# Transposing x and q by DMA instead of on TensorE in a sorted block attention with a maxout layer

## The chip, the cores and the metric

The kernel runs on one core of a Trainium2 chip. The metric is the time of one execution on the device, in microseconds (us); for the kernel before it is 178.51 us, the median of three runs (178.17 to 178.69). A profile of one execution, which spans 176.5 us on the core, gives what each engine did and when. The engines are TensorE (PE in the profile, with its weight loads as PEld), VectorE (DVE), ScalarE (ACT), GpSimd (POOL) and SyncE (SP); SP here only issues transfers. Matmul results land in PSUM, of which this kernel makes four buffers, and some other engine has to move ("evict") each to SBUF.

## The reference, cut to what matters

Four items (the batch), eight heads, 768 tokens, head size 64. Each head's tokens fall into 8 blocks of 96. A small matrix P (8x8 for each head, made doubly stochastic by five rounds) mixes the blocks of k and of v; then each block of queries attends to its mixed block; the result is, token by token, the x of a layer with two input matrices, a maximum, and an output matrix.

```python
for _ in range(5):
    P = P - np.max(P, axis=-1, keepdims=True)
    P = np.exp(P)
    P = P / (np.sum(P, axis=-1, keepdims=True) + 1e-09)
    P = P / (np.sum(P, axis=-2, keepdims=True) + 1e-09)
k_sorted = np.einsum('bhij,bhjcd->bhicd', P, k_b)      # the same for v
scores = scale * np.matmul(q_b, k_sb.transpose(0, 1, 2, 4, 3))
attn = softmax(scores)                                  # written out in the reference
x = np.matmul(attn, v_sb)                               # -> (4*768 tokens, 512)
h1 = x @ w1
h2 = x @ w2
out = np.maximum(h1, h2) @ w_out
```

## The kernel before

The kernel uses max(h1, h2) = relu(x(w1-w2)) + x w2, so the output is relu(x(w1-w2)) w_out + x (w2 w_out). All products are bf16. The program is a fixed order of instructions: for each item, 20 or 24 "units" on TensorE (eight products h, twelve halves of output tiles; item one has four products of weights as well), and between the units "steps" of the attention of the next item. The parts that the change touches (cuts are marked `...`):

```python
# queries: paired by heads on VectorE, transposed on TensorE, evicted
def pair_q(b, two):
    if two == 0:
        q_pair[b] = qpool.tile([128, HP, R, 2 * D], BF16, tag="q_pair", name="q_pair", bufs=1)
    nc.vector.tensor_copy(out=q_pair[b][..., two * D : (two + 1) * D], in_=...)  # q_raw[b]

def q_transposes(b, half, eng=None, n=0):
    ...
    for m in range(2 * R):                       # 12 of 128x128
        ...
            nc.tensor.matmul(ps[:, c], q_pair[b][:, hp, r], ident, is_transpose=True, ...)
    ...
    evac(qT[b][:, half * 2 : half * 2 + 2]..., ps[:, 0 : 2 * R * 128], ...)

# scores of four blocks and two heads, then the exponent
def scores(b, u, n=0):
    ih, hp = divmod(u, HP)
    ps = ps_f32("s_ps")
    ...
            rhs = qT[b][rows, hp, :, i * PB : (i + 1) * PB]      # R x PB = 6 x 16 tokens
            nc.tensor.matmul(
                ps[:, h2 * 512 + ii * BLK : h2 * 512 + (ii + 1) * BLK],
                kT[b][rows, ...], rhs, start=True, stop=True,
            )
    e = e_bufs[(b * 8 + u) % NE]
    nc.scalar.activation(out=e[...], in_=ps[0:BLK]..., func=AF.Exp, scale=scale)

# values; x is divided by the sum of its row as it leaves PSUM
def values(b, u, n=0):
    ...   # 8 matmuls o_ps <- e, v_sb
    nc.vector.reciprocal(out=rs, in_=ov[:, :, :, 64])
    if hp % 2 == 0:
        x_tiles[b, ih, hp // 2] = xpool.tile([BLK, 2, 4, 2, D], BF16, tag="x", name="x", bufs=3)
    ...
    nc.vector.tensor_tensor(out=x, in0=ov[:, :, :, 0:D], in1=rs..., op=ALU.mult)

# x transposed on TensorE; its eviction puts the tokens in order
def x_transposes(b, t, eng=None):
    ih, hh = divmod(t, 2)
    ps = ps_bf16("tx_ps")
    x = x_tiles.pop((b, ih, hh))
    for m in range(8):                           # 8 of 96x128
        ...
    dst = xT[:, b % 2, ih, hh].rearrange("p h (i c r) -> p h i c r", r=R, c=PB)
    src = ps.rearrange("p (h f) -> p h f", h=2)[:, :, 0:TCH].rearrange("p h (i r c) -> p h i c r", r=R, c=PB)
    evac(dst, src, 2 * TCH, eng=eng)

# products h of unit t of chunk ch (384 tokens): reads w1_sb and xT, evicted as g
def moe_h_products(b, ch, t, hps, n=0): ...
# half an output tile of 128 tokens: reads g and wo_sb, xT and wc
def moe_out(b, ti, part): ...                    # every fourth half evicts o and stores it from SP

# the order: steps of the next item, and what hangs behind a unit by its number
tail = {..., 9: [pair_q(1, 0), pair_q(1, 1), load_q(2), load_v(2), load_v(3)],
        16: [block_diagonals(2)], 18: [block_diagonals(3)]}       # lambdas left out
for b in range(B):
    ...
    tail = {0: [VA[6], VA[7]], 1: [TR[2]], 2: [TR[3]]}            # behind the next item's first units
    if b == 0:
        tail[3] = [load_k(3)]
        tail[8] = [load_q(3)]
```

SC, VA and TR are the scores (8 for an item), values (8) and transposes of x (4; the first two feed chunk 0, the others chunk 1). Items are numbered from 0 in the code; the text says item one for b = 0. Bulk loads of q, k, v and the weights go from GpSimd's queue and cast fp32 to bf16 on the way; the stores of the output go from SP's.

Of the kernel before, what the change touches and what calls it, by code (L numbers as in the profile page):

```python
# [9 lines left out]

FP32 = mybir.dt.float32
BF16 = mybir.dt.bfloat16


@with_exitstack
def kernel(
# [16 lines left out]
    nc = tc.nc  # L33
# [4 lines left out]
    B, H, S, D = q.shape  # L38
    NB = sort_net.shape[-1]
    BLK = S // NB  # L40
# [5 lines left out]
    R = S // 128  # L46
    PB = 128 // NB
    HP = H // 2
    HB = BLK // 2
    TCH = S // 2  # L50
# [152 lines left out]
    def turn_v(rows, eng, c0, c1, d0=0, d1=D):  # L203
        dst = v_dc[rows, 0 : D * BLK].rearrange("p (d c) -> p d c", c=BLK)[:, d0:d1, c0:c1]
        src = v_raw[rows].rearrange("p (c d) -> p d c", d=D)[:, d0:d1, c0:c1]
        if eng == "A":
            nc.scalar.copy(out=dst, in_=src)
        else:
            nc.vector.tensor_copy(out=dst, in_=src)  # L209


    rowsum = const.tile([G, NB], FP32, tag="rowsum", name="rowsum")
# [116 lines left out]
        )  # L329
        load["D"] += 900  # L330

    def q_transposes(b, half, eng=None, n=0):

        if half == 0:
            qT[b] = qpool.tile([128, HP, R, 128], BF16, tag="qT", name="qT")
        ps = ps_f32("tq_ps") if n else ps_bf16("tq_ps")
        keep_streaming(ps, n)
        if n:
            ps = ps.bitcast(BF16)
        for m in range(2 * R):  # L340
            hp, r = half * 2 + m // R, m % R
            c = slice(m * 128, (m + 1) * 128)
            if b in q_pair:
                nc.tensor.matmul(  # L344
                    ps[:, c], q_pair[b][:, hp, r], ident, is_transpose=True, start=True, stop=True
                )
                continue
            for h2 in range(2):
                nc.tensor.matmul(  # L349
                    ps[h2 * 64 : h2 * 64 + 64, c],  # L350
                    q_raw[b][:, hp + 4 * h2, r * D : (r + 1) * D],
                    ident,
                    is_transpose=True,
                    start=True,
                    stop=True,
                )
# [78 lines left out]
        keep_streaming(ps, n)  # L435
        for ii in range(4):
            i = ih * 4 + ii
            for h2 in range(2):
                rows = slice(h2 * 64, h2 * 64 + 64)
                rhs = qT[b][rows, hp, :, i * PB : (i + 1) * PB]  # L440
                nc.tensor.matmul(  # L441
                    ps[:, h2 * 512 + ii * BLK : h2 * 512 + (ii + 1) * BLK],
                    kT[b][rows, (hp * 8 + i) * BLK : (hp * 8 + i) * BLK + 128],
                    rhs,
                    start=True,
                    stop=True,
                )
        e = e_bufs[(b * 8 + u) % NE]
        nc.scalar.activation(  # L449
            out=e[:, 0 : 8 * BLK].rearrange("p (t f) -> p t f", t=2),  # L450
            in_=ps[0:BLK].rearrange("p (t f) -> p t f", t=2)[:, :, 0 : 4 * BLK],
            func=AF.Exp,
            scale=scale,
        )
        load["A"] += 800
        e_tiles[b, u] = e

    def values(b, u, n=0):
        ih, hp = divmod(u, HP)
        e = e_tiles.pop((b, u))  # L460
        m0 = (b % 2) * 64
        ps = ps_f32("o_ps")
        keep_streaming(ps, n)
        for h2 in range(2):
            for ii in range(4):
                nc.tensor.matmul(  # L466
                    ps[:, h2 * 512 + ii * 65 : h2 * 512 + (ii + 1) * 65],
                    e[:, (h2 * 4 + ii) * BLK : (h2 * 4 + ii) * BLK + 128],
                    v_sb[:, m0 + (hp + 4 * h2) * 8 + ih * 4 + ii, 0:65],
                    start=True,  # L470
                    stop=True,
                )
        ov = ps[0:BLK].rearrange("p (t f) -> p t f", t=2)[:, :, 0 : 4 * 65].rearrange(
            "p t (i f) -> p t i f", f=65
        )
        rs = xpool.tile([BLK, 2, 4], FP32, tag="rs", name="rs")
        nc.vector.reciprocal(out=rs, in_=ov[:, :, :, 64])  # L477
        if hp % 2 == 0:
            x_tiles[b, ih, hp // 2] = xpool.tile(
                [BLK, 2, 4, 2, D], BF16, tag="x", name="x", bufs=3  # L480
            )
        x = x_tiles[b, ih, hp // 2][:, :, :, hp % 2, :]
        nc.vector.tensor_tensor(  # L483
            out=x,
            in0=ov[:, :, :, 0:D],
            in1=rs.to_broadcast([BLK, 2, 4, D]),
            op=ALU.mult,
        )
        load["D"] += 900

    def x_transposes(b, t, eng=None):

        ih, hh = divmod(t, 2)
        ps = ps_bf16("tx_ps")
        x = x_tiles.pop((b, ih, hh))
        for m in range(8):
            h2, ii = divmod(m, 4)
            nc.tensor.matmul(  # L498
                ps[:, h2 * 1024 + ii * BLK : h2 * 1024 + (ii + 1) * BLK],
                x[:, h2, ii].rearrange("p n d -> p (n d)"),  # L500
                ident[0:BLK, 0:BLK],
                is_transpose=True,
                start=True,
                stop=True,
            )
# [192 lines left out]
    def load_rest():  # L698
# [18 lines left out]
        9: [  # L717
            lambda: pair_q(1, 0),
            lambda: pair_q(1, 1),
            lambda: load_q(2),  # L720
            lambda: load_v(2),
            lambda: load_v(3),
        ],
        16: [lambda: block_diagonals(2)],
        18: [lambda: block_diagonals(3)],
    }
    for b in range(B):
        units = [lambda t=t: moe_h(b, 0, t, None if b else "A") for t in range(4)]
        if b == 0:
# [21 lines left out]
            ]  # L751
        steps, lo = [], 2
        if b < B - 1:
            qs = [lambda half=half: q_transposes(b + 1, half) for half in range(2)]
            pairs = [lambda two=two: pair_q(b + 1, two) for two in range(2)]
            ks = [lambda t=t, b=b: sort_k(b + 1, t) for t in range(3)]
            SC, VA, TR = att(b + 1)

            def group(*fs):
                return [lambda: [f() for f in fs]]  # L760

            if b == 0:
                lo = 10
                tail[9][2:2] = ks
                vs = [lambda t=t: sort_v(1, t) for t in range(4)]
                tns = [lambda c=c: turn(both, c) for c in range(0, BLK, 12)]
                VA[1:6] = [(lambda f=f, g=g: (f(), g())) for f, g in zip(VA[1:6], tns)]
                TR[0:2] = [(lambda f=f, g=g: (f(), g())) for f, g in zip(TR[0:2], tns[5:])]
                SC[7:] = [lambda f=SC[7], g=tns[7]: (f(), g())]
                steps = group(*vs[:3]) + qs[:1] + group(*SC[0:2], vs[3]) + qs[1:] + VA[:1]  # L770
                steps += group(*SC[2:5]) + VA[1:2]
            elif b == 1:
                vs = [lambda t=t: sort_v_pair(2, t) for t in range(8)]
                steps = group(*pairs) + group(*ks) + qs[:1] + group(*SC[0:2], vs[0]) + qs[1:]
                steps += group(*vs[1:4]) + group(*vs[4:7]) + group(*SC[2:4], vs[7]) + VA[:2]
            else:
                steps = group(*pairs) + group(*ks) + qs + group(*SC[0:2])
# [19 lines left out]
_INS = ['q', 'k', 'v', 'sort_net', 'moe_w1', 'moe_w2', 'moe_w_out']  # L797
_OUTS = [((3072, 512), 'float32')]
# [25 lines left out]
```

The softmax here doesn't subtract the row's maximum and nothing guards it: scores larger than these inputs give would overflow.

## Time and profile before

| what | value |
|---|---|
| time, median of 3 runs | 178.51 us |
| span of the profiled execution | 176.5 us |
| granted TensorE clock | 1.00 throughout |
| matmuls L593 (output tiles) | 208 + 104 instructions, 48.1 + 25.0 us busy |
| matmuls L566 (h) | 256 instructions, 45.8 us busy |
| matmuls L498 (transposes of x) | 128 instructions, 8.1 us busy |
| matmuls L344 and L349 (transposes of q) | 72 and 48 instructions, 4.8 and 1.7 us busy |
| exponents on ScalarE, L449 | 32 instructions, 24.2 us busy |
| moved from and to HBM | 25.17 MB read, 6.29 MB written |

How to read it: "busy" adds the durations of an engine's instructions, where overlapping ones count once. Matmuls are pipelined: the next begins before the one ahead of it has ended, so a group's mean duration is longer than what one more of its kind adds to the time. A row of a group reads: line of the kernel, engine, operation, output <- inputs, shapes, count | busy us, mean ns of one | idle us of the engine just ahead of them, and what ended most of that idle time. The chain of work that ended last is followed back from the last instruction, at each step to what released it, or to the instruction ahead of it on its engine. Row "DMA" of the slices gives in tenths how busy the 16 DMA engines were in each fortieth of the span.

### The profile page before, as it was taken

The page shows a single profiled execution, that of the slowest core. Times are in us where ns is not written, and L with a number is a line of the kernel's source. Part 1 is how long each engine was busy: PE and PEld are TensorE (multiplying, and loading weights), DVE is VectorE, ACT ScalarE, POOL GpSimd, SP SyncE. Part 2 cuts the span into 40 slices and gives each one's busy share as a digit, 9 for nine tenths or more (in the row PEclk, how much of TensorE's full clock was granted, in tenths as well). Part 3 has the DMA queues.
Part 4 walks back from the last instruction along what each step waited for, and adds up shares of the span by engine and source line. Part 5 has one row for each costly group of instructions (what it writes and reads, how often), then busy time and mean ns, then how long its engine had stood idle before and what let it go on. Part 6 is the DMA issues. An engine that isn't in the chain of part 4 may idle for free.

```text
span 176.5 us, 4808 instructions
## 1 busy us (share of the span) xinstructions
PE 169.4 (96%) x2159; PEld 105.1 (60%) x2159; DVE 95.3 (54%) x201; ACT 91.1 (52%) x110; POOL 24.1 (14%) x39
## 2 busy tenths in 40 slices
PE   7999999999999999999989999999999999999993
PEld 7848675655765554577655454677555546654453
DVE  4979758688555697354586435346325426240210
ACT  3689957854663655277783341474833232630021
POOL 7855353110730000020000000000000000000000
PEclk9999999999999999999999999999999999999999
DMA  4999999999799962039200203300001132000333
GB/s 55 200 205 208 198 207 215 201 203 210 114 214 212 206 176 108 16 119 148 38 0 4 97 26 119 119 6 4 0 0 62 61 119 111 12 0 0 119 116 125
DMA packets 13940, 19.19 MB, mean 109 GB/s; under 512 B 800, under 2 KB 8864, under 8 KB 13920
## 3 DMA queue, kind: packets, MB, share of 16 engines
q0 software_dynamic: 10304, 12.58, 42.4%
q1 hardware_dynamic: 3328, 6.10, 9.1%
q8 instruction: 17, 0.28, 0.6%
q10 hardware_dynamic: 288, 0.20, 0.3%
q14 instruction: 3, 0.02, 0.0%
HBM read 25.17 MB, written 6.29 MB: 178 GB/s over the span
## 4 chain that ended last, share of the span: by engine, by line
PE 84%; DVE 9%; ACT 4%; issue 1%; DMA 1%; ACTq 0%
PE out_ps L593 36%; PE h_ps L566 23%; PE o_ps L466 4%; PE k_ps L374 4%; PE wc_ps L544 4%; PE tx_ps L498 3%; PE s_ps L441 3%; PE tq_ps L344 2%; PE v_ps L395 2%; DVE g L582 1%; ACT w2T L103 1%; PE tw_ps L521 1%; DMA p_sb<-in_sort_net_dram 1%; PE tq_ps L349 1%; DVE x L483 1%
## 5 line engine op out<-in xcount | busy, mean ns | idle before, releaser
L593 PE MATMUL out_ps<-wo_sb,g 128*128 128x512 bf16 (+2 forms) x208 | 48.1, 363 | 0.3 <-DVE g L582 0.2
L566 PE MATMUL h_ps<-xT,w_sb 128*128 128x384 bf16 x256 | 45.8, 326 | 0.4 <-DVE g L582 0.2
L566 PEld LDWEIGHTS <-w_sb 128*128 128x128 bf16 x256 | 23.8, 98 | 15.1 <-issue 0.2
L449 ACT ACTIVATE e<-s_ps 96x768 bf16<-96x768 f32 x32 | 24.2, 803 | 12.2 <-PE s_ps L441 12.0
L580 ACT ACTIVATE g<-h_ps 128x768 bf16<-128x768 f32 x22 | 17.7, 811 | 21.8 <-PE h_ps L566 21.7
L593 PEld LDWEIGHTS <-g 128*128 128x128 bf16 x208 | 17.9, 97 | 15.9 <-issue 0.2
L593 PE MATMUL out_ps<-wc,xT 128*128 128x512 bf16 (+2 forms) x104 | 25.0, 362 | 0.0
L103 ACT COPY o<-out_ps 128x1024 f32<-128x1024 f32 x8 | 8.1, 1013 | 29.3 <-PE out_ps L593 25.6
L483 DVE TENSOR_TENSOR x<-o_ps,rs 96x512 bf16<-96x512 f32 x32 | 22.0, 687 | 1.1
L477 DVE RECIPROCAL rs<-o_ps 96x8 f32<-96x8 f32 x32 | 6.4, 201 | 25.5 <-PE o_ps L466 25.4
L582 DVE TENSOR_SCALAR g<-h_ps 128x768 bf16<-128x768 f32 x10 | 9.6, 957 | 15.7 <-PE h_ps L566 15.6
L593 PEld LDWEIGHTS <-xT 128*128 128x128 bf16 x104 | 9.9, 97 | 10.9
L209 DVE COPY v_dc<-v_raw 64x768 bf16<-64x768 bf16 (+2 forms) x18 | 15.6, 897 | 0.5 <-DMA v_raw<-in_v_dram 0.4
L466 PEld LDWEIGHTS <-e 96*128 96x128 bf16 x256 | 11.0, 98 | 5.6 <-ACT e L449 0.5
L466 PE MATMUL o_ps<-v_sb,e 96*128 96x65 bf16 x256 | 12.4, 193 | 0.3 <-DVE x L483 0.2
L103 ACT COPY xT<-tx_ps 128x768 bf16<-128x768 bf16 x13 | 10.4, 798 | 4.5 <-PE tx_ps L498 4.5
L105 DVE CAST v_sb<-v_ps 96x1024 bf16<-96x1024 f32 x7 | 8.5, 1215 | 5.3 <-PE v_ps L395 3.3
L103 ACT CAST v_sb<-v_ps 96x1024 bf16<-96x1024 f32 x9 | 8.7, 1014 | 2.3 <-PE v_ps L395 1.4
L103 ACT CAST kT<-k_ps 128x1024 bf16<-128x1024 f32 x10 | 9.6, 1026 | 0.5 <-PE k_ps L374 0.5
L441 PEld LDWEIGHTS <-kT 64*128 64x128 bf16 x256 | 6.1, 94 | 5.4 <-issue 4.6
L129 POOL DMA_DIRECT2D q_raw<-in_q_dram x4 | 3.6, 902 | 39.8 <-DVE q_pair L326 37.4
L81 PEld LDWEIGHTS <-fill 128*128 128x128 bf16 x109 | 7.7, 128 | 2.2 <-DVE fill L72 1.2
(77 smaller groups left out, 166.1 us busy)
## 6 DMA issues: line engine op xcount, KB each, us to landing
out_dram<-o SPq DMA_DIRECT2D x11, 512.0 KB, 2.8
k_raw<-in_k_dram POOLq DMA_DIRECT2D x12, 256.0 KB, 14.0
q_raw<-in_q_dram POOLq DMA_DIRECT2D x4, 768.0 KB, 9.7
v_raw<-in_v_dram POOLq DMA_DIRECT2D x6, 384.0 KB, 12.5
w_sb<-in_moe_w_dram POOLq DMA_DIRECT2D x3, 512.0 KB, 15.7
wo_sb<-in_moe_w_out_dram POOLq DMA_DIRECT2D x2, 512.0 KB, 19.4
v_raw<-in_v_dram POOLq DMA_DIRECT2D x3, 256.0 KB, 5.1
w_sb<-in_moe_w_dram POOLq DMA_DIRECT2D x2, 256.0 KB, 14.3
```

Of the source, the lines that this page charges most:

```text
L81: nc.tensor.matmul(ps[:, 0:w], w0, fill[:, 0:w], start=True, stop=True)
L103: nc.scalar.copy(out=out_ap, in_=in_ap)
L105: nc.vector.tensor_copy(out=out_ap, in_=in_ap)
L209: nc.vector.tensor_copy(out=dst, in_=src)
L441: nc.tensor.matmul(ps[:, h2 * 512 + ii * BLK : h2 * 512 + (ii + 1) * BLK], kT[b][rows, (hp * 8 + i) * BLK : (hp * 8 + i) * BLK + 128], rhs ...
L449: nc.scalar.activation(out=e[:, 0 : 8 * BLK].rearrange("p (t f) -> p t f", t=2), in_=ps[0:BLK].rearrange("p (t f) -> p t f", t=2)[:, :, 0 ...
L466: nc.tensor.matmul(ps[:, h2 * 512 + ii * 65 : h2 * 512 + (ii + 1) * 65], e[:, (h2 * 4 + ii) * BLK : (h2 * 4 + ii) * BLK + 128], v_sb[:, m0 ...
L483: nc.vector.tensor_tensor(out=x, in0=ov[:, :, :, 0:D], in1=rs.to_broadcast([BLK, 2, 4, D]), op=ALU.mult,)
L566: nc.tensor.matmul(h_ps[t][:, m * 512 : m * 512 + TCH], w1_sb[:, hp, fb * 128 : (fb + 1) * 128], xT[:, b % 2, ch, hp % 2, hp // 2, :], sta ...
L580: nc.scalar.activation(out=g, in_=src, func=AF.Relu)
L582: nc.vector.tensor_scalar(out=g, in0=src, scalar1=0.0, scalar2=None, op0=ALU.max)
L593: nc.tensor.matmul(dst, g_tiles[b, ch, m // 2][:, m % 2, off : off + 128] if m < NFB else xT[:, b % 2, ch, hp % 2, hp // 2, off : off + 12 ...
```

## The change

For items two to four the normalised x, and for items three and four the queries, no longer go through TensorE and an eviction: a DMA from the SP queue transposes them from SBUF to SBUF. It is meant to relieve TensorE of the transposes, and VectorE and ScalarE of their evictions. [...]the exponent now reads the scores in the order of tokens. Around this the order is changed: the transposes are started as early as their data is there, the last two values of an item are computed ahead of the item boundary, the loads of v for items three and four go ahead of the q of item three, and the loads of k and q of item four wait for the first scores of item three, so that no bulk load runs near the transposes. `TWICE = 1` leaves the copies of v as they are.

```diff
-    def q_transposes(b, half, eng=None, n=0):
+    def q_transposes(b, half, eng=None):
 
         if half == 0:
             qT[b] = qpool.tile([128, HP, R, 128], BF16, tag="qT", name="qT")
-        ps = ps_f32("tq_ps") if n else ps_bf16("tq_ps")
-        keep_streaming(ps, n)
-        if n:
-            ps = ps.bitcast(BF16)
+        if b > 1:
+            nc.sync.dma_start_transpose(
+                out=qT[b][:, half * 2 : half * 2 + 2].rearrange("p h r c -> p (h r) c"),
+                in_=q_pair[b][:, half * 2 : half * 2 + 2].rearrange("p h r e -> p (h r e)"),
+            )
+            return
+        ps = ps_bf16("tq_ps")
... scores
-                    ps[:, h2 * 512 + ii * BLK : h2 * 512 + (ii + 1) * BLK],
+                    ps[:, h2 * 512 + ii * 128 : h2 * 512 + ii * 128 + BLK],
...
-            out=e[:, 0 : 8 * BLK].rearrange("p (t f) -> p t f", t=2),
-            in_=ps[0:BLK].rearrange("p (t f) -> p t f", t=2)[:, :, 0 : 4 * BLK],
+            out=e[:, 0 : 8 * BLK].rearrange("p (t c r) -> p t c r", t=8, r=R),
+            in_=ps[0:BLK].rearrange("p (t f) -> p t f", t=8)[:, :, 0:BLK].rearrange(
+                "p t (r c) -> p t c r", r=R
+            ),
... values
-                [BLK, 2, 4, 2, D], BF16, tag="x", name="x", bufs=3
+                [BLK, 2, 4, 2, D], BF16, tag="x", name="x", bufs=4
... x_transposes
+        if b > 0:
+            nc.sync.dma_start_transpose(
+                out=xT[:, b % 2, ih, hh].rearrange("p h (i c) -> p (h i) c", c=BLK),
+                in_=x.rearrange("p h i n d -> p (h i n d)"),
+            )
+            return
...
-        dst = xT[:, b % 2, ih, hh].rearrange("p h (i c r) -> p h i c r", r=R, c=PB)
-        src = ps.rearrange("p (h f) -> p h f", h=2)[:, :, 0:TCH].rearrange(
-            "p h (i r c) -> p h i c r", r=R, c=PB
-        )
-        evac(dst, src, 2 * TCH, eng=eng)
+        src = ps.rearrange("p (h f) -> p h f", h=2)[:, :, 0:TCH]
+        evac(xT[:, b % 2, ih, hh], src, 2 * TCH, eng=eng)
... the order
-            lambda: load_q(2),
             lambda: load_v(2),
             lambda: load_v(3),
+            lambda: load_q(2),
         ],
-        16: [lambda: block_diagonals(2)],
-        18: [lambda: block_diagonals(3)],
+        22: [lambda: block_diagonals(2)],
+        23: [lambda: block_diagonals(3)],
     }
+    def late_loads():
+
+        held = const.tile([1, 1], BF16, tag="held", name="held")
+        nc.gpsimd.tensor_copy(out=held, in_=e_tiles[2, 0][0:1, 0:1])
+        load_k(3)
+        load_q(3)
...
-            pairs = [lambda two=two: pair_q(b + 1, two) for two in range(2)]
+            if b < 2:
+                tail[18 - 4 * b] = [lambda two=two: pair_q(b + 2, two) for two in range(2)]
+                tail[18 - 4 * b] += [lambda half=half: q_transposes(b + 2, half) for half in range(2)]
...
-                steps = group(*pairs) + group(*ks) + qs[:1] + group(*SC[0:2], vs[0]) + qs[1:]
+                steps = group(*ks) + group(*SC[0:2], vs[0], late_loads)
...
-            steps += VA[2:3] + TR[:1] + VA[3:4]
-            steps += group(*rest[:-1]) + TR[1:2] + VA[4:5] + rest[-1:] + VA[5:6]
+            steps[-1:] = group(VA[1], TR[0])
+            steps += VA[2:3] + group(VA[3], TR[1])
+            steps += group(*rest[:-1]) + VA[4:5] + rest[-1:] + group(VA[5], TR[2])
+            steps += VA[6:7] + group(VA[7], TR[3])
...
-        tail = {0: [VA[6], VA[7]], 1: [TR[2]], 2: [TR[3]]}
-        if b == 0:
-            tail[3] = [lambda: load_k(3)]
-            tail[8] = [lambda: load_q(3)]
+        tail = {}
```

More of the change, by code (lines that the diff above doesn't have):

```diff
@@ L12 @@
 BF16 = mybir.dt.bfloat16
+TWICE = 1
 @with_exitstack
@@ L205, in turn_v @@
         src = v_raw[rows].rearrange("p (c d) -> p d c", d=D)[:, d0:d1, c0:c1]
[L206 to L209, printed above, removed]
+        for _ in range(TWICE):
+            if eng == "A":
+                nc.scalar.copy(out=dst, in_=src)
+            else:
+                nc.vector.tensor_copy(out=dst, in_=src)
     rowsum = const.tile([G, NB], FP32, tag="rowsum", name="rowsum")
@@ L493, in x_transposes @@
         ih, hh = divmod(t, 2)
+        x = x_tiles.pop((b, ih, hh))
+        if b > 0:
[4 more added lines that the diff above has]
+            return
         ps = ps_bf16("tx_ps")
-        x = x_tiles.pop((b, ih, hh))
         for m in range(8):
@@ L753 @@
         if b < B - 1:
-            qs = [lambda half=half: q_transposes(b + 1, half) for half in range(2)]
-            pairs = [lambda two=two: pair_q(b + 1, two) for two in range(2)]
+            qs = [lambda half=half: q_transposes(1, half) for half in range(2)]
+            if b < 2:
+                tail[18 - 4 * b] = [lambda two=two: pair_q(b + 2, two) for two in range(2)]
+                tail[18 - 4 * b] += [lambda half=half: q_transposes(b + 2, half) for half in range(2)]
             ks = [lambda t=t, b=b: sort_k(b + 1, t) for t in range(3)]
@@ L773 @@
                 vs = [lambda t=t: sort_v_pair(2, t) for t in range(8)]
-                steps = group(*pairs) + group(*ks) + qs[:1] + group(*SC[0:2], vs[0]) + qs[1:]
+                steps = group(*ks) + group(*SC[0:2], vs[0], late_loads)
                 steps += group(*vs[1:4]) + group(*vs[4:7]) + group(*SC[2:4], vs[7]) + VA[:2]
             else:
-                steps = group(*pairs) + group(*ks) + qs + group(*SC[0:2])
+                steps = group(*ks) + group(*SC[0:2])
                 steps += VA[:1] + group(*SC[2:5]) + VA[1:2]
             rest = SC[4:] if b == 1 else SC[5:]
-            steps += VA[2:3] + TR[:1] + VA[3:4]
-            steps += group(*rest[:-1]) + TR[1:2] + VA[4:5] + rest[-1:] + VA[5:6]
+            steps[-1:] = group(VA[1], TR[0])
+            steps += VA[2:3] + group(VA[3], TR[1])
+            steps += group(*rest[:-1]) + VA[4:5] + rest[-1:] + group(VA[5], TR[2])
+            steps += VA[6:7] + group(VA[7], TR[3])
         done = 0
```

## The prediction

> **What bounds the kernel now.** I read the busy table and the slices first, then the chain of work that ended last, then the groups, and last the DMA issues. The busy table, and the slices of the same page:
>
> ```profile
> PE 169.4 (96%) x2159; PEld 105.1 (60%) x2159; DVE 95.3 (54%) x201; ACT 91.1 (52%) x110; POOL 24.1 (14%) x39
> ...
> PE   7999999999999999999989999999999999999993
> ...
> DMA  4999999999799962039200203300001132000333
> ```
>
> TensorE is full in every slice but the first and the last; VectorE and ScalarE are half idle; the DMA engines are full until about 62 us (14 slices of 4.4 us), and after that in spells: a load of q at 79 to 84 us, and the stores. Matmul busy time is overlapping time, so 96% alone doesn't say that TensorE is the bound. The chain does:
>
> ```profile
> PE 84%; DVE 9%; ACT 4%; issue 1%; DMA 1%; ACTq 0%
> PE out_ps L593 36%; PE h_ps L566 23%; PE o_ps L466 4%; PE k_ps L374 4%; PE wc_ps L544 4%; PE tx_ps L498 3%; PE s_ps L441 3%; PE tq_ps L344 2%; PE v_ps L395 2%; DVE g L582 1%; ACT w2T L103 1%; PE tw_ps L521 1%; DMA p_sb<-in_sort_net_dram 1%; PE tq_ps L349 1%; DVE x L483 1%
> ```
>
> Most of the DVE share is the Sinkhorn start (the first 12.6 us). After it, the set end is TensorE work laid end to end, and the transposes (L498 of x, L344 of q) are links of that chain, not work beside it. The same chain in order of time, around the start of item two (start, us, what):
>
> ```profile
> 75.22 1.30 PE h_ps L566 x8
> 76.52 0.34 PE tx_ps L498 x8
> 76.86 1.30 PE h_ps L566 x8
> 78.16 0.34 PE tx_ps L498 x8
> 78.50 1.64 PE k_ps L374 x96
> 80.14 1.41 PE h_ps L566 x8
> 81.55 0.67 PE tq_ps L344 x12
> ```
>
> Here a transpose costs its steady price: eight of x take 0.34 us (42 ns each), twelve of q 0.67 us (56 ns), with nothing idle before or behind. These are the prices to use, not the groups' mean of about 0.2 us for one, which contains its latency.
>
> **What the Trainium skill says.** (1) "VectorE: DVE Perf Modes", section "The three transpose paths", gives a 128x128 bf16 transpose 390 ns on TensorE and 1309 ns by the DMA crossbar. Back to back this trace has 56 ns for the first, seven times less: the page's figure is for one alone. A DMA transpose has no trace here. (2) "DMA: Bandwidth & Descriptors", section "Latency and other measured facts", gives DMA transposes 261 GB/s with a non-contiguous middle dimension. No run shows this yet. (3) The same page, section "Rules for kernel authors": issue a DMA early and wait late, so that its fixed cost overlaps; and a transpose beside ordinary DMAs needs no ordering. The trace agrees with a fixed cost, in the last row of these DMA issues (KB each, median us from issue to landing):
>
> ```profile
> out_dram<-o SPq DMA_DIRECT2D x11, 512.0 KB, 2.8
> ...
> p_sb<-in_sort_net_dram SPq DMA_DIRECT2D x1, 8.0 KB, 1.7
> ```
>
> An 8 KB load on the SP queue needs 1.7 us, nearly all of it fixed.
>
> **The change part by part.** Removed from TensorE: the transposes of x for three items, 3 x 4 calls of 8, 12 x 0.34 = 4.1 us; those of q for two items, 2 x 2 calls of 12, 4 x 0.67 = 2.7 us (the chain has 0.67, 0.67 and 1.34). All of it lies on the path. Sum 6.8 us.
>
> Removed from the half-idle engines, with the evictions' own rows:
>
> ```profile
> L103 ACT COPY xT<-tx_ps 128x768 bf16<-128x768 bf16 x13 | 10.4, 798 | 4.5 <-PE tx_ps L498 4.5
> ...
> L105 DVE COPY qT<-tq_ps 128x1536 bf16<-128x1536 bf16 x7 | 6.6, 953 | 1.8 <-PE tq_ps L344 1.1 <-PE tq_ps L349 0.7
> ```
>
> Twelve evictions of xT (0.80 us on ScalarE, 0.95 on VectorE) and four of qT (0.95, one of them 1.44 on ScalarE), some 14 us over the two engines. It is worth time only where TensorE waits for a PSUM buffer. Between 83 and 91 us the chain leaves TensorE three times for an eviction of g (0.82, 0.97, 0.97 us); TensorE has scores and sorted values to run meanwhile, so it stands idle only 0.2 to 0.3 us each time. Two qT evictions fall in this stretch, but the transposes that kept TensorE busy go too. I credit 0.3 us.
>
> Added: the SP queue gets 12 transposes of 96x1024 (197 KB) and 4 of 128x1536 (393 KB). Estimated from the 1.7 us above and the page's 261 GB/s: 1.7 + 0.75 = 2.5 us and 1.7 + 1.5 = 3.2 us. Off the path, if the result isn't needed sooner. The tightest consumers, with times of the kernel before:
> - Last x of item two. Its values now run ahead of the last two halves of an output tile, about 70.6 us; by the row of x (687 ns) behind such a call it is ready at 71.9. Its reader is the fifth product h of item two, at 84.4, or about 82.4 when the transposes and the two moved calls of values in between are taken out. Slack 10 us.
> - x for the first chunk of item two: ready near 62.8, read at 73: slack 10 us.
> - q of item three: paired near 66.9, read by the scores near 82: slack 15 us.
> If the queue moves one transpose at a time, with T for an x and 2T for a q half, four T of q and two of x stand between 66.9 and some 80.6 us (1.8 us of landing left over): T may be up to 2.3 us, that is 197 KB / 2.3 us = 85 GB/s. The page's rate is three times that. Item three gives nearly the same (q paired near 105, last x read near 119.5), and item four has no q behind it.
>
> Changed without cost: the exponent now reads PSUM with a step of 16 fp32, where it read in order (803 ns for 768). The eviction of kT reads with a step of 64 fp32 and takes 1026 ns for 1024 elements, the one of o reads in order and takes 1013: on ScalarE the step costs nothing here. The eviction of item one's xT becomes an ordered one, 0.80 us as before.
>
> Moved: the values of the last two units go ahead of the item boundary, 2 x 0.24 us merely moved. The loads of v for items three and four go ahead of q for item three: the two v are 1.5 MB, q 0.8 MB, issued from about 45 us; at the 205 GB/s of those slices they are through at 45 + 11.5 + 2 = 58.5 us, just ahead of the first DMA transpose (x ready near 59.7), and q is used at 65. k and q of item four wait for the first scores of item three (about 82 us), and need 1.5 MB / 205 GB/s = 7.5 us more with 2.6 us of issuing: landed near 92 to 94, while q is paired near 100. So no new wait from loads.
>
> Sum: 178.5 - 6.8 - 0.3 = 171.4 us. As some of the slack is estimated and new groupings cost a pipeline break of 0.1 us here and there, I say 172.0.
>
> **Rivals.** (a) The DMA transposes are much slower than the page says. For it: nothing in the trace shows one, rows of 256 bytes and 96 partitions may suit the engines badly, and the author keeps bulk loads away from them, which looks like something learned. Against: the slack of a factor of three, and DMA engines that are little used from 66 us on. With T = 4 us, the row of six T ends at 66.9 + 24 + 1.8 = 93 against 82.4: 10 us lost before item two's second chunk and, with a similar row, as much in item three, some 190 us in all. T = 3 us loses about 4 each time: 180.
> (b) The SP queue also carries the output stores. A store behind a waiting or slow transpose keeps its o buffer (three of them, one store every 5 us), then ScalarE's eviction, then a PSUM buffer of TensorE. It takes some 10 us of delay to do harm; short of (a) it costs nothing. 175 if it bites a little.
> (c) TensorE is no longer the bound at the starts of items three and four, where evictions come thick: at most the 6.8 us shrink by the TensorE time that was hidden under evictions, about 1 us. 172.5.
> (d) Better than the sum: fewer PSUM users remove all g waits of item three and the break at 127 us, another 1 us. 170.4.
>
> **Range and chances.** The sum with (c) and (d) spans 170 to 173; (a) in its mild form and (b) stretch upward to 179. Faster by over 2% means under 174.9. I give the page's order of magnitude for the crossbar, with its threefold slack, two chances in three; the rest is divided between a mild and a heavy wait. Predicted 172.0 us, 169.8 to 179.0; faster 0.67, within 2% 0.16, slower 0.17.
>
> **What would show it.** Right: L498 matmuls fall from 128 to 32, L344 from 72 to 24; the chain remains TensorE nearly throughout, its DMA share stays at 1%; an x transpose lands in 2 to 4 us; the first products h of each item follow the outputs with no gap; the exponent stays at 0.80 us. Wrong: waits of h (L566) or s for xT or qT from a DMA; transposes that queue up over 66 to 82 us; waits of SP or of o's eviction for stores; an exponent of over 0.9 us, which with 32 of them would fill ScalarE further; pairings of q that wait for their load.

## The result and the profile after

The changed kernel takes 173.72 us (median of 4 runs, 173.26 to 174.08) against 178.53 us: 0.9732 of the time before (95% interval 0.9704 to 0.976). It is faster by 4.8 us, where the prediction said 6.5 (172.0 us, range 169.8 to 179.0).

First the page of the changed kernel: busy time, the slices of TensorE and of the DMA engines, and the chain that ended last.

```profile
PE 161.7 (94%) x1997; PEld 98.1 (57%) x2015; DVE 88.4 (51%) x194; ACT 83.8 (49%) x101; POOL 24.5 (14%) x40
...
PE   7899999989999999998989899999999999999990
...
DMA  3999999999999352993497549920035173000342
...
PE 79%; DMA 7%; ACT 6%; POOL 2%; DVE 2%; issue 2%; ACTq 0%; POOLq 0%
```

TensorE is still full, but three slices between 78 and 99 us now show an eight, where the kernel before had one such slice. The DMA share of 7% in the chain is the load of q of item one at the very start (the chain's other line gives `DMA q_raw<-in_q_dram 7%`), which happened to end last before 16.8 us; no DMA transpose stands in the chain. Three rows of the DMA issues (KB each, median us from issue to landing) and the row of the exponent:

```profile
out_dram<-o SPq DMA_DIRECT2D x11, 512.0 KB, 3.0
...
xT<-x SPq DMA_TRANSPOSE x12, 2.9
...
qT<-q_pair SPq DMA_TRANSPOSE x4, 4.0
```

```profile
L454 ACT ACTIVATE e<-s_ps 96x768 bf16<-96x768 f32 x32 | 24.2, 807 | 15.8 <-PE s_ps L446 15.7
```

The transposes land in 2.9 and 4.0 us, and the exponent with its strided read takes 807 ns (803 before).

Where the time went shows best by item, from the first product h of one item to that of the next (read in the timelines of TensorE). "Worked out" is what the prediction's own prices say: 0.34 us for eight transposes of x, 0.67 for a half of q, 0.24 for a moved call of values.

| stretch | before | after | difference | worked out |
|---|---|---|---|---|
| start to first h of item two | 73.27 | 73.34 | +0.07 | -0.19 |
| item two | 37.81 | 36.29 | -1.52 | -2.70 |
| item three | 35.24 | 32.34 | -2.90 | -2.70 |
| products h of item four | 11.58 | 10.40 | -1.18 | -1.17 |
| outputs of item four to the end | 18.6 | 19.9 | +1.3 | 0 |
| span | 176.5 | 172.3 | -4.2 | -6.8 |

Items three and four gave what was worked out (item three 0.2 us more). Item two gave 1.2 us less, and the end grew by 1.3 us. Two waits of TensorE that the kernel before does not have lie in item two (engine, line, waited for: us in total, times, longest), the first in its products h, the second among its outputs:

```profile
PE s_ps L446 <- ACT kT L104: 0.6, 1, 0.6
PE out_ps L603 <- ACT o L104: 0.5, 1, 0.5
```

The chain of the changed kernel in order of time (start, us, what) in the products h of item two:

```profile
77.45 0.81 ACT g L590
78.26 2.75 ACT kT L104 x3
81.01 0.05 issue
81.05 0.51 PE s_ps L446 x16
81.57 0.23 PE v_ps L421 x16
81.80 1.44 PE h_ps L576 x8
83.24 0.02 issue
83.26 0.82 ACT g L590
84.08 0.04 issue
84.12 1.47 PE h_ps L576 x8
85.59 0.02 issue
85.62 0.97 DVE g L592
86.59 0.04 issue
86.63 1.48 PE h_ps L576 x8
```

From 77 us on evictions are links between the matmuls: three kT in a row on ScalarE, then a g behind each product. Busy time in that stretch (columns: length, then busy us and count for PE, PEld, DVE, ACT, POOL, then clock, DMA share, GB/s), first the kernel before, then the changed one:

```profile
73.30:91.40 18.10, 17.47 (x345) 12.56 (x344) 9.72 (x14) 13.81 (x16) 0.90 (x1) 1.00 0.40 74
```

```profile
73.40:90.60 17.20, 15.90 (x327) 10.56 (x327) 7.28 (x9) 14.23 (x17) 2.68 (x5) 1.00 0.73 154
```

ScalarE has 14.2 us of work in 17.2, VectorE 7.3; before it was 13.8 and 9.7 in 18.1. So ScalarE's load in this stretch has not fallen, although evictions were removed: two calls of scores (32 matmuls s_ps instead of 16) and one unit of sorted values (128 matmuls v_ps instead of 112) that had stood among the outputs now stand here. The kernel picks the engine of an eviction by running totals over the whole program, not by what is due now.

The experiments had to answer four things: are the transposes worth their chain price; why does item two give less; how much room do the DMA transposes have; and what of the end. My theory ahead of them: the DMA transposes are hidden, and the q transposes of item three had stood in a stretch that waits for evictions anyway, so taking them out brought nothing. The rivals: a part of the DMA transposes is waited for; or the new order costs nothing and TensorE's prices were too high.

### The profile page after: what moved, and what is told of

Read it like the earlier page. It is cut to its first block, busy times and chain, and to the rows that moved or that the text cites. A ratio compares the mean times of both kernels' runs of the same rounds, so it can differ in the third digit from the quotient of the medians.

```text
span 172.3 us, 4531 instructions
## 1 busy us (share of the span) xinstructions
PE 161.7 (94%) x1997; PEld 98.1 (57%) x2015; DVE 88.4 (51%) x194; ACT 83.8 (49%) x101; POOL 24.5 (14%) x40
## 4 chain that ended last, share of the span: by engine, by line
PE 79%; DMA 7%; ACT 6%; POOL 2%; DVE 2%; issue 2%; ACTq 0%; POOLq 0%
PE out_ps L603 36%; PE h_ps L576 24%; DMA q_raw<-in_q_dram 7%; PE o_ps L473 5%; PE wc_ps L554 4%; PE s_ps L446 3%; PE k_ps L379 2%; ACT kT L104 2%; ACT g L590 1%; DVE g L592 1%; ACT w2T L104 1%; PE tw_ps L531 1%; PE tq_ps L349 1%; PE tq_ps L354 1%; POOL k_raw L145 1%
## 5 line engine op out<-in xcount | busy, mean ns | idle before, releaser
L603 PE MATMUL out_ps<-wo_sb,g 128*128 128x512 bf16 (+2 forms) x197 | 47.0, 362 | 1.1 <-ACT o L104 0.5
L576 PE MATMUL h_ps<-xT,w_sb 128*128 128x384 bf16 x256 | 44.8, 326 | 0.8 <-DVE g L592 0.6
L104 ACT COPY o<-out_ps 128x1024 f32<-128x1024 f32 x10 | 10.1, 1012 | 31.4 <-PE out_ps L603 31.4
L473 PEld LDWEIGHTS <-e 96*128 96x128 bf16 x256 | 11.6, 97 | 6.6 <-DVE x L490 0.5
L473 PE MATMUL o_ps<-v_sb,e 96*128 96x65 bf16 x256 | 13.1, 193 | 0.1
L446 PE MATMUL s_ps<-qT,kT 64*128 64x96 bf16 x256 | 8.7, 204 | 0.7 <-ACT kT L104 0.6
L104 ACT CAST kT<-k_ps 128x1024 bf16<-128x1024 f32 x9 | 8.6, 1021 | 0.7 <-PE k_ps L379 0.7
L554 PE MATMUL wc_ps<-wo_sb,w2T 128*128 128x512 bf16 x29 | 7.4, 380 | 0.7 <-ACT w2T L104 0.5
## 6 DMA issues: line engine op xcount, KB each, us to landing
w_sb<-in_moe_w_dram POOLq DMA_DIRECT2D x2, 256.0 KB, 14.3
```

Source lines behind the costliest of these rows:

```text
L104: nc.scalar.copy(out=out_ap, in_=in_ap)
L446: nc.tensor.matmul(ps[:, h2 * 512 + ii * 128 : h2 * 512 + ii * 128 + BLK], kT[b][rows, (hp * 8 + i) * BLK : (hp * 8 + i) * BLK + 128], rhs ...
L473: nc.tensor.matmul(ps[:, h2 * 512 + ii * 65 : h2 * 512 + (ii + 1) * 65], e[:, (h2 * 4 + ii) * BLK : (h2 * 4 + ii) * BLK + 128], v_sb[:, m0 ...
L554: nc.tensor.matmul(wc_ps[0][:, m * 512 : (m + 1) * 512], w2T[:, fb, dmt * 128 : (dmt + 1) * 128], wo_sb[:, fb, :], start=(fb == 0), stop=( ...
L576: nc.tensor.matmul(h_ps[t][:, m * 512 : m * 512 + TCH], w1_sb[:, hp, fb * 128 : (fb + 1) * 128], xT[:, b % 2, ch, hp % 2, hp // 2, :], sta ...
L603: nc.tensor.matmul(dst, g_tiles[b, ch, m // 2][:, m % 2, off : off + 128] if m < NFB else xT[:, b % 2, ch, hp % 2, hp // 2, off : off + 12 ...
```

## Experiments: each kind of transpose put back

**x on TensorE again**, with the order of calls in which each follows its values by one step; q stays with the DMA.

```diff
-        if b > 0:
+        if b > 9:
             nc.sync.dma_start_transpose(      # x
...
-            steps[-1:] = group(VA[1], TR[0])
-            steps += VA[2:3] + group(VA[3], TR[1])
-            steps += group(*rest[:-1]) + VA[4:5] + rest[-1:] + group(VA[5], TR[2])
-            steps += VA[6:7] + group(VA[7], TR[3])
+            steps[-1:] = group(VA[1])
+            steps += group(VA[2], TR[0]) + group(VA[3])
+            steps += group(*rest[:-1], TR[1]) + VA[4:5] + rest[-1:] + group(VA[5])
+            steps += group(VA[6], TR[2]) + group(VA[7])
...
-        tail = {}
+        tail = {0: [TR[3]]} if b < B - 1 else {}
```

> The changed kernel (173.7 us) with x of items two to four transposed on TensorE again and evicted, each transpose one step behind its values; q stays with the DMA. If x's transposes lie on the path at their chain price, 12 x 0.34 = 4.1 us come back: 177.4 to 177.9 us. Rival: in item two, where TensorE now waits for evictions, the transposes fit into the waits, and only some 3 us come back: 176.7 us or less. Second question, the end: the stores after the last eviction took 3.9 us in the profile of the changed kernel against 2.5 before; if the DMA transposes of x have to do with that, it falls back to 2.5 here.

Measured: 178.09 us (177.94 to 178.53), 4.4 us more than the changed kernel. That is a little over the expected span and far from the rival.

**q of items three and four on TensorE again**, a unit behind its pairing; x stays with the DMA.

```diff
-        if b > 1:
+        if b > 9:
             nc.sync.dma_start_transpose(      # q
...
-                tail[18 - 4 * b] += [lambda half=half: q_transposes(b + 2, half) for half in range(2)]
+                for half in range(2):
+                    tail.setdefault(19 - 4 * b + half, []).append(
+                        lambda b=b, half=half: q_transposes(b + 2, half)
+                    )
```

> The changed kernel with q of items three and four transposed on TensorE, among the output halves where it now starts (a unit behind its pairing); x stays with the DMA. If every q transpose costs its chain price there, 4 x 0.67 = 2.7 us come back: 176.2 to 176.5 us. Rival: its place doesn't matter and part of it was hidden before as well; then 175.5 or less.

Measured: 176.16 us (176.09 to 176.23), 2.4 us more, near the chain price of 2.7 for four.

**Both on TensorE**: order, loads and exponent of the changed kernel, no DMA transpose.

> Order, loads and exponent of the changed kernel, but all transposes on TensorE: no DMA transpose at all. Theory: removing the transposes is worth its 6.8 us and the rest of the change costs 1 to 2 us, because q of item three left a stretch in which TensorE waits for evictions anyway: 179.5 to 180.5 us, slower than the kernel before (178.5). Rival: the new order is free (178.5 us) and the transposes by DMA bring only 4.8 us because something of them is waited for. End of the kernel: 2.5 us from the last eviction on if the DMA transposes lengthen it, up to 3.9 if that is chance.

Measured: 180.35 us (180.30 to 180.48), 1.0116 of the kernel before (1.0102 to 1.013). So with nearly the same order the DMA transposes bring 180.35 - 173.72 = 6.6 us, where the prediction had 6.8, and the rest of the change, with the transposes on TensorE, costs 180.35 - 178.39 = 2.0 us. The rival falls: the order is not free.

That the sums come so near to the prices is in part luck. The changed kernel's end, from the last eviction on, is about 1 us longer than in these three (see the experiment on the end). From the first product h of item one to the end of the last eviction, against the profile of the changed kernel run again (145.10 us), x costs 5.4 us, q 3.3 and both 7.8, more than the prices. The excess is largely waits that come with the transposes here: with x put back TensorE waits 1.0 us for an x that stands behind copies of v on VectorE, with q alone put back 0.6 us for a pairing of q. The changed kernel has neither wait. So the 2.0 us are not what the order costs the changed kernel, which loses the 1.2 us of item two and the longer end.

## Experiments: what the transposes of q were worth in their old place

**Idle matmuls in the old place of q of item three** in the changed kernel: twice 1,536 columns of zeros into a scratch buffer.

```diff
-                steps = group(*ks) + group(*SC[0:2], vs[0], late_loads)
-                steps += group(*vs[1:4]) + ...
+                fill_q = lambda: keep_streaming(ps_f32("fill_ps"), 1536, width=128)
+                steps = group(*ks) + group(fill_q, *SC[0:2], vs[0], late_loads)
+                steps += group(fill_q, *vs[1:4]) + ...
```

> The changed kernel with idle matmuls on TensorE (zeros, into a scratch PSUM buffer, twice 12 of 128 columns, 2 x 0.64 us) in the products h of item two where the kernel before transposed q of item three. Theory: from 77 to 91 us TensorE waits for evictions, so the transposes that stood there before cost almost nothing, and taking them out brought almost nothing: the time rises by at most 0.5 us, 173.6 to 174.2. Rival: TensorE is the bound there as well, and what the change lost is lost elsewhere: the full 1.3 us, 175.0 us or more.

Measured: 173.17 us (173.10 to 173.31), no more than the changed kernel. In the profile the last eviction ends at 168.93 us instead of 168.44, so 0.5 of the 1.3 us arrive there, and the stores behind it are shorter (below). TensorE had room for the other 0.8 us.

**The kernel before with q of item three alone by DMA**, paired among the outputs of item one; the load of q of item four is held back by a copy on GpSimd that reads a g of item two. **The kernel before with q of item four alone by DMA**, paired among the outputs of item two. Both use the same branch, with `b == 2` in the first and `b == 3` in the second:

```diff
+        if b == 2:
+            nc.sync.dma_start_transpose(out=qT[b]..., in_=q_pair[b]...)
+            return
...
-        18: [lambda: block_diagonals(3)],
+        18: [lambda: block_diagonals(3), lambda: pair_q(2, 0), lambda: pair_q(2, 1),
+             lambda: q_transposes(2, 0), lambda: q_transposes(2, 1)],
...
-                steps = group(*pairs) + group(*ks) + qs[:1] + group(*SC[0:2], vs[0]) + qs[1:]
+                steps = group(*ks) + group(*SC[0:2], vs[0])
```

> The kernel before, with q of item three alone paired and transposed by DMA among the outputs of item one (as the changed kernel does), and the load of q of item four held back until the fourth product h of item two so that it doesn't meet them; x and all else as before. This takes two q transposes out of the products h of item two. Theory: TensorE has idle time for them there, so the time stays: 178.0 to 178.5 us (0 to 0.4 us less). Rival, as the prediction had it: they lie on the path, 2 x 0.67 = 1.3 us less, 177.0 us.

> The kernel before, with q of item four alone paired and transposed by DMA among the outputs of item two; this takes two q transposes out of the products h of item three, where no sorted values are evicted. Theory: here they lie on the path, 1.3 us less: 176.9 to 177.3 us. Rival: the chain price is too high for q in general; then less than 0.7 us, as for item three.

Measured: 178.51 us for item three (1.0012 of the kernel before, 1.0002 to 1.0022) and 177.01 us for item four (0.9924, 0.9911 to 0.9937; 1.3 us less). The same two calls (24 transposes), removed in two places, are worth nothing in one and their full price in the other. By item it is the same: item two takes 37.56 us instead of 37.81 in the first, item three 33.56 instead of 35.24 in the second. With the transposes go their evictions and their place in the order, so these two runs price the whole removal. The chain of the first of these kernels shows what took the place of the transposes:

```profile
78.02 0.81 ACT g L586
78.83 0.69 ACT xT L103
79.52 2.76 ACT kT L103 x3
82.28 0.05 issue
82.33 0.52 PE s_ps L447 x16
82.84 0.23 PE v_ps L422 x16
83.08 1.42 PE h_ps L572 x8
84.50 0.02 issue
84.52 0.97 DVE g L588
```

Where a q transpose stood behind the keys, the scores now wait for the kT evictions, the same picture as in the changed kernel.

## Experiments: the evictions of that stretch

**One kT of item three on VectorE** (`eng='D'` for the second of its three).

> The changed kernel, with the second of the three kT evictions of item three put on VectorE (all three run one after another on ScalarE, 78.2 to 81.0 us, and the scores wait for the last). Theory: TensorE waits for evictions at the start of item two's products, so the wait of the scores (0.6 us) goes and ScalarE gets to the next evictions 1 us sooner: 172.6 to 173.2 us. Rival: the wait moves to the next eviction of g or v_sb, and the time stays at 173.5 to 173.8 us.

Measured: 173.99 us (173.22 to 174.14), no gain. The rival holds: the wait of the scores is gone, but TensorE waits 0.6 us for g and 0.3 us for v_sb on ScalarE. The running totals answered the move by giving ScalarE one more v_sb (five instead of four), so its load stayed at 14.3 us and VectorE's at 7.3; the run did not lighten ScalarE.

**The sorted values spread singly**, evictions dealt out in turn.

```diff
+                vs = [lambda t=t, e=e: sort_v_pair(2, t, e) for t, e in enumerate("DADAADDA")]
+                ks = [lambda t=t, e=e: sort_k(2, t, eng=e) for t, e in enumerate("DAD")]
+                tail[0], tail[1] = [vs[0]], [vs[1]]
+                steps = group(*ks) + group(*SC[0:2], late_loads)
+                steps += group(*vs[2:4]) + group(*vs[4:6]) + group(*vs[6:8], *SC[2:4]) + VA[:2]
```

> The changed kernel, with the eight sorted-value units of items three and four spread (two in the first two products h of item two, then two behind a product instead of three), and the evictions of that stretch dealt out in turn over ScalarE and VectorE. Each product then has about 1.8 us of TensorE work against 1.5 us of evictions on two engines. Theory (the stretch is bound by evictions that come in lumps): the excess of 1.7 us in this stretch goes, 171.9 to 172.6 us. Rival (the stretch is bound by something else, e.g. the pipeline of one product after the other): 173.5 us or more.

Measured: 173.68 us (173.52 to 174.31), no gain either. Its chain has few evictions left in this stretch, but each product pays for a change of kind:

```profile
73.30 1.41 PE h_ps L576 x8
74.70 0.34 PE v_ps L421 x16
75.05 1.41 PE h_ps L576 x8
76.45 0.34 PE v_ps L421 x16
76.79 1.41 PE h_ps L576 x8
```

A product h behind another takes 1.30 us, behind sorted values 1.41, and a unit of sixteen sorted values alone 0.34, where it took 0.23 behind its like. ScalarE's load did fall here, to 12.0 us; but two more such changes than in the changed kernel, and a wait of 0.4 us for v_sb, leave 0.2 us of gain in this stretch (17.16 us from the first h to the first output, 17.34 in the changed kernel). And the running totals, now different, picked engines for item three that cost 0.6 us in its products h (14.97 us against 14.39).

**The sorted values in lumps, but evictions dealt out**: three units ahead of the keys, then three and two; engines in turn; the running totals are set afterwards to what they were.

```diff
+                vs = [lambda t=t, e=e: sort_v_pair(2, t, e) for t, e in enumerate("ADAADAAD")]
+                ks = [lambda t=t, e=e: sort_k(2, t, eng=e) for t, e in enumerate("ADA")]
+                tail[1] = vs[0:3]
+                tail[8] = [lambda: load.update(A=50800.0, D=50866.666)]
+                steps = group(*ks) + group(*SC[0:2], late_loads)
+                steps += group(*vs[3:6]) + group(*vs[6:8]) + group(*SC[2:4]) + VA[:2]
... products h of item two: engines of their evictions
+                "ADDD" for the first four, "DDAD" for the others
```

> The changed kernel; three of the eight sorted-value units go ahead of the sorted keys, and the evictions of this stretch are dealt out in turn over ScalarE and VectorE (in the changed kernel ScalarE has 14.4 us of work in these 17.4, VectorE 7.3); the balance that picks engines afterwards is set to what it was. Theory: ScalarE is what TensorE waits for there, so 0.7 to 1.5 us go: 172.2 to 173.0 us. Rival: as where the units were spread one by one, TensorE's own changes between kinds of matmuls eat it: 173.4 us or more.

Measured: 172.25 us (171.98 to 172.56), 0.9656 of the kernel before (0.9643 to 0.9669): the fastest kernel here, 1.0 us ahead of the changed kernel run beside it (173.22). The same stretch in it:

```profile
73.00:90.00 17.00, 16.42 (x329) 10.65 (x331) 10.51 (x13) 12.30 (x14) 2.67 (x5) 1.00 0.65 139
```

ScalarE 12.3 us, VectorE 10.5; from the first h to the first output it takes 16.67 us instead of 17.34, and the products h of item three keep their 14.39. The stretch thus gives back 0.7 us, the low end of the expected span, with the same matmuls in it, and the wait of the scores for kT is gone. A shorter end adds to it: 2.9 us in this profile, 3.6 in that of the changed kernel run beside it. The vanished wait, 0.6 us, says that ScalarE's evictions were most of what the products h of item two had lost; how much of the 0.7 us is due to the three units moved ahead was not tried apart. The wait of 0.5 us for o among the outputs of item two is in this kernel as well; no run removed it.

## Experiments: how much room the DMA transposes have

**Each DMA transpose twice**, the second into a scratch tile.

```diff
+            again = xpool.tile([128, 8, BLK], BF16, tag="again_x", name="again", bufs=2)
+            nc.sync.dma_start_transpose(
+                out=again, in_=x.rearrange("p h i n d -> p (h i n d)")
+            )
... and the same behind each half of q
```

> The changed kernel with every DMA transpose issued a second time right behind the first, into a scratch tile that nothing reads (393 KB per x, 786 KB per q half in all). Theory (the transposes are wholly hidden, with some 10 us of slack): a transpose holds the SP queue 1.2 to 2 us, so the row of two q halves and two x before the second chunk of item two ends about 6 us later, near 83 us, where the products need it: at most 1 us more, 173.7 to 174.8. Rival (the transposes are on the edge already): each item loses several us, 178 or more.

Measured: 175.14 us (174.29 to 176.77), 1.4 to 1.9 us more than the changed kernel (173.72, and 173.22 when it was run again). Now TensorE does wait for a transpose:

```profile
PE h_ps L585 <- DMA xT<-x: 1.7, 2, 1.5
```

The room is used up at about twice the transposes, a little sooner than expected. One eviction of o also waits 4.7 us for an earlier store, the sign of the prediction's rival (b), but no wait of TensorE follows from it. With the transposes as they are neither wait is in the profile.

**A bulk load beside the transposes**: nine needless loads of 768 KB, each released by the x that is transposed at the same moment.

```diff
+        if b > 0 and t > 0:
+            gate = const.tile([1, 1], BF16, tag=f"gate{b}{t}", name="gate")
+            nc.gpsimd.tensor_copy(out=gate, in_=x[0:1, 0, 0, 0, 0:1])
+            near = qpool.tile([128, H, R * D], BF16, tag="near", name="near", bufs=2)
+            nc.gpsimd.dma_start(out=near, in_=q[0].rearrange("h (p r) d -> p h (r d)", r=R))
```

> The changed kernel with a needless bulk load of 768 KB (q of item one again, into a scratch tile) started beside each transpose of x but an item's first, nine in all. What is the keeping away of bulk loads worth? Theory: the transposes share the DMA engines with the load and land after 5 to 10 us instead of 2.9 (x) and 4.0 (q); the slack of about 10 us swallows most of it, 173.7 to 175.5 us. Rival: the loads starve the transposes, each lands only when the load is through or later, waits pile up in all three items: 178 us or more.

Measured: 201.75 us in the fastest of four executions, up to 207.76 in the others (205.91 in the profiled one): the rival holds, and the loss is 28 us or more. The wait of TensorE, then the landings:

```profile
PE h_ps L581 <- DMA xT<-x: 27.5, 5, 12.1
```

```profile
xT<-x SPq DMA_TRANSPOSE x12, 8.6
...
qT<-q_pair SPq DMA_TRANSPOSE x4, 14.1
```

A transpose of x lands after 8.6 us in the median and 17.0 at most, a half of q after 14.1. The SP queue itself is held up, as its timeline shows (start, us, what):

```profile
67.35 8.48 SPq L339 DMA_TRANSPOSE qT<-q_pair  x2
75.87 0.58 SPq L628 DMA_DIRECT2D out_dram<-o  x1
76.50 10.74 SPq L508 DMA_TRANSPOSE xT<-x  x2
```

Issuing these two pairs takes 8.5 and 10.7 us; the changed kernel needs 4.1 and 3.5. As they go one after another on the queue, the delay adds up until x for the second chunk of item two arrives at 98.75 us. The expectation took the landing of x about right (5 to 10 us) and that of q too low, and forgot that they add up in a row of four. Nine loads are far more than the change moves out of the way (the loads of k and q of item four, and the order of v and q), so this run shows that bulk loads have to be kept away from the transposes, not what those few would have cost.

## Experiment: the end

In the profile of the changed kernel the stores behind the last eviction took longer. The last store's issue in the changed kernel, and in the one with idle matmuls (start, us, what):

```profile
168.46 1.09 ACTq L639 DMA_DIRECT2D out_dram<-o  x1
```

```profile
168.95 0.34 ACTq L639 DMA_DIRECT2D out_dram<-o  x1
```

That store lands 2.9 us after its issue in the first and 1.6 in the second and in the kernel before. From the end of the last eviction to the end of the span it takes 172.3 - 168.44 = 3.9 us in the first and 171.5 - 168.93 = 2.6 us in the second; before 2.5. So the changed kernel was run once more:

> The changed kernel itself once more, beside the others on the same chip. Its stores at the end took 3.9 us from the last eviction on in its profile, 2.5 to 3.8 in kernels that differ from it elsewhere, 2.5 to 2.7 with few or no DMA transposes. If the long end belongs to it, this look has it again (3.5 us or more); if it is chance, it may come out at 2.5, and the time nearer to 173.2 than to 174.1 us.

Measured: 173.22 us (172.78 to 173.72), with 3.6 us at its end. The long end came again. Over all profiles: 2.5 to 3.0 us in the six kernels with none to twelve DMA transposes; with 16 or more, and no extra loads, 3.9 and 3.6 (the changed kernel), 3.8 (values spread), 3.1 (twice), 3.0 (kT), 2.9 (lumps) and 2.6 us (idle matmuls). More than 3.0 was seen only with all the DMA transposes, but the same number of them can end without it. What decides it, no run here shows; it is left open. It is worth up to 1.3 us.

## Why the prediction was right, and where it was off

- **The bound, and the 6.8 us removed from TensorE.** Right: with the transposes put back the time is 6.6 us longer (x 4.4, q 2.4 each alone), though this closeness is in part luck, as said above. "All of it lies on the path" was wrong for one part: q of item three, 1.3 us. Removed alone from the kernel before it changed nothing (178.51), while q of item four brought its 1.3. The chain of the kernel before showed both as links of the same size; it did not show that behind the one the wait for an eviction only begins later.
- **"I credit 0.3 us" for the evictions removed**, and "merely moved" for the order. This is the step that failed: instead of a gain of 0.3 us, item two falls 1.2 us short. 0.7 us of it lie in its products h, where the removed steps pulled scores and sorted values forward, so that ScalarE kept its 14 us of work while TensorE's shrank; with the evictions dealt out the 0.7 us came back. The other 0.5 us have the length of the one wait for o among the outputs; that this wait is the cause is not shown by a run. The stretch had been read by TensorE's idle moments, 0.2 to 0.3 us each, and not by the load of the two evicting engines.
- **Rival (c)** had named the kind and the size, "about 1 us" of TensorE time hidden under evictions, though for the starts of items three and four; it came in item two, while the attention of item three is worked out. It should have stood in the sum.
- **The DMA transposes.** 2.5 and 3.2 us were estimated from an 8 KB load and the 261 GB/s of the Trainium skill ("DMA: Bandwidth & Descriptors", section "Latency and other measured facts"); measured 2.9 and 4.0. The second 197 KB of a q half take 4.0 - 2.9 = 1.1 us, an estimate of 180 GB/s if all of the difference is transfer, below the page's 261. Hidden, as said. "Slack 10 us" and the threefold margin were generous: twice the transposes cost 1.4 us or more. Rival (a) fell for transposes alone, but its hint, that bulk loads do harm, was right: TensorE waits 27.5 us when they meet. The skill's rule that a transpose beside ordinary DMAs needs nothing (same page, section "Rules for kernel authors") is about which transfers must wait for one another and says nothing of time; in time, x beside a bulk load landed after 8.6 us instead of 2.9.
- **Stores behind transposes, rival (b).** No wait of TensorE or of an eviction for a store in the middle of the changed kernel; one of 4.7 us with twice the transposes. The longer end was not foreseen.
- **Exponent and loads.** Right: the exponent, which now does the reordering of tokens that the eviction of x did, takes 807 ns against 803, and the pairings of q of items three and four did not wait for their loads (66.6 and 100.5 us, expected near 65 and 100).

The predicted 172.0 was low by 1.7 us. Item two accounts for 1.2 and the end for about 1; the 0.3 us credited did not come; the 0.6 us that had been added to the sum for small breaks made up for a part of this, which is luck.

## What to carry to other kernels

A link in the chain is worth its length only if the engine that waits behind it isn't due to wait anyway: before pricing a removal, add up the load of the evicting engines in that stretch, and if it is as uneven as here (14.2 and 7.3 us in 17.2), deal the evictions out first. Moving transposes to a DMA queue was a real gain for this kernel, bound by TensorE, with the consumers several times the landing time away and no bulk load beside them; hold loads back by a dependency on something that the computation produces. Transposes in a row on one queue add up, so it is the row, not one landing, that must fit into the slack.

## What the runs showed of the hardware that was not expected

- A DMA transpose of x, which lands after 2.9 us in the median (4.7 at most) in the changed kernel, took 8.6 us in the median and up to 17.0 with bulk loads of 768 KB beside it; its issue held the queue for up to 5.4 us, where it is 1.3 us in the median and 2.5 at most in the changed kernel.
- While TensorE stood idle in that run, its granted clock fell to 0.50 (windows of 5 us, columns as above; this view's DMA share passes 1 here):

```profile
75.00:80.00 5.00, 5.00 (x117) 3.29 (x115) 0.00 (x0) 4.02 (x6) 0.00 (x0) 1.00 1.29 193
80.00:85.00 5.00, 0.82 (x33) 0.63 (x32) 1.22 (x1) 2.71 (x4) 2.60 (x5) 0.76 1.34 160
85.00:90.00 5.00, 0.00 (x0) 0.00 (x0) 0.00 (x0) 0.00 (x0) 0.10 (x1) 0.50 1.34 174
```

- Eight 128x384 products take 1.30 us behind their like and 1.41 behind 64-row matmuls: about 0.1 us for each change of kind.
- The end of the kernel after the last eviction took 3.6 to 3.9 us in three profiles with 16 DMA transposes, 2.5 us in the two kernels without any, for a cause that stayed open.
